# Moving 36 tile transposes from TensorE to the DMA crossbar, and the Q head masks from VectorE to GpSimd, in a transformer block bound by its exps

## The chip, the cores and the metric

One core of one Trainium2 chip. The metric is the device time of one execution in microseconds (us), as a median of several. Executions of one kernel mostly agree within 0.3%; each is marked fast or slow, and only fast ones are compared. Engines: PE is TensorE (matrix products and transposes), DVE is VectorE, ACT is ScalarE, POOL is GpSimd, SP is SyncE, which here only issues DMAs.

## The reference

A transformer block on one sequence of S = 2048 tokens, D = 512, with H = 32 heads of 16, and a gated FFN with F = 1792; all in bf16.

```python
def _A_ref(x, wqkv, wo):                       # attention
    qkv = (x @ wqkv).reshape(B, S, 3, H, Dh).transpose(2, 0, 3, 1, 4)
    q, k, v = qkv[0], qkv[1], qkv[2]
    scores = einsum("bhqd,bhkd->bhqk", q, k) * (Dh ** -0.5)
    p = softmax(scores)
    o = einsum("bhqk,bhkd->bhqd", p, v)
    return o.transpose(0, 2, 1, 3).reshape(B, S, D) @ wo
def _B_ref(x, w_gate, w_up, w_down):           # FFN
    return (gelu(x @ w_gate) * (x @ w_up)) @ w_down

h = x + _A_ref(layernorm(x), wqkv, wo)         # LN1
return h + _B_ref(layernorm(h), w_gate, w_up, w_down)   # LN2
```

With 32 heads of width 16, the scores are 2048 tiles of 128 keys x 512 queries, and every element needs an exp. That is the kernel's bulk.

## The kernel before

The kernel is a list scheduler in Python. Each piece of work is a generator that yields operations with a modelled duration, and asks for PSUM banks with `Acquire` (PSUM is the memory that PE's products are written to, here in eight banks of 128 x 512 floats); the scheduler decides, when the program is built, the order of the instructions on each engine. On the chip this order is fixed, and engines wait for one another by semaphores.

The exps are shared. ACT takes two tiles per step, from PSUM banks 0 to 3 (`pbank`), into `PT`:

```python
yield Op("act", TEXP(n), ACTF(PT[:, p0:p0 + n, :], pbank[:, b0:b0 + n, :], ACT.Exp, scale=LN2 / 1024, bias=math.log(PSCALE)), ...)
```

DVE takes the rest whenever the scheduler finds room, in groups of four tiles:

```python
# dconv, per tile: PSUM -> uint16
yield Op("dve", 0.603, lambda e: e.tensor_scalar(out=dXE[...][:, 0, j, :], in0=pbank[:, b, :], ...))
# dchain, per group of n tiles: mantissa, exponent, product
yield Op("dve", t1, lambda e: e.tensor_scalar(out=W.bitcast(U16), in0=X, ...), reads=kX, writes=kW, port=True)   # W is dW
yield Op("dve", t1, lambda e: e.tensor_scalar(out=E, in0=X, ...), reads=kX, writes=kE, port=True)
yield Op("dve", t2, lambda e: e.tensor_tensor(out=X.bitcast(F16), in0=W, in1=X.bitcast(F16), op=ALU.mult), reads=kW + kX, writes=kX, port=True)
```

So less other work on DVE lets the scheduler hand more tiles to DVE, and ACT gets fewer steps. Where PE would idle, the scheduler puts dummy matmuls (`zero_bf`).

Three kinds of tile are transposed by PE into a PSUM bank and copied out by DVE: the 16 tiles of LN1, the 16 of the attention output (`Otok`) and the 16 of LN2 (`hn_sb`, the same memory as `OnT`). One of them, the others look alike:

```python
b = yield Acquire(reads=rd, gate=lambda: C["oproj"] >= first_t[c])
pt = pbank[:, b, :].bitcast(BF16)
yield Op("pe", 4 * TTR, cols=512, fns=[lambda e, hc=hc: e.transpose(out=pt[:, 128 * hc:128 * hc + 128], in_=Otok[:, cp, qt, 128 * hc:128 * hc + 128], identity=ident[:])
                     for hc in range(4)], reads=rd, writes=[("pb", b)])
yield copy_op(c, qt, OnT[:, qt, :, :], pt[:, 0:512].rearrange("p (c s) -> p c s", c=4), reads=[("pb", b)], writes=[("OH", qt)])
```

Q leaves PSUM twice, since one matmul of 32 rows serves two heads of 16 and each head needs a copy in which the other's rows are zero:

```python
for par in range(2):
    ...                                        # (the first ones on ACT)
    yield Op("dve", 0.66, lambda e, par=par: e.tensor_scalar(out=QT[:, c, 2 * j + par, :], in0=pbank[:, b, :], scalar1=qmask[:, par:par + 1], scalar2=None, op0=ALU.mult), ...)
proj_done(b)
```

Of the kernel before, what the change touches and what calls it, by code (L numbers as in the profile page):

```python
# [1093 lines left out]
TAIL = dict(pe=0.17, act=0.13, dve=0.083)  # L1094
LATS = {("pe", "act"): 0.04, ("pe", "dve"): 0.04, ("act", "pe"): 0.058, ("dve", "pe"): 0.06, ("dve", "dve"): 0.034, ("act", "act"): 0.04, ("pool", "pool"): 0.05}
PVM = 2
SLOTS = ((0, 2), (2, 2))
PVB = 4
DENSE = (5, 6, 7)
# [62 lines left out]
def fast_path(nc, P, base0, ARENA, pbank, flag, A_x, A_wqkv, A_wo, B_x, B_w_gate, B_w_up, B_w_down, out):  # L1162
# [25 lines left out]
    xn_sb = at("xn_sb", [128, 8, D], BF16)  # L1188
    GUT = at("GUT", [128, NFC, 512], BF16, offE)
    offF = cur[0]  # L1190
    xnT = at("xnT", [128, 4, S], BF16)
    wqkv_sb = at("wqkv_sb", [128, 4, 3 * D], BF16)
    wg_sb = at("wg_sb", [128, 4, F], BF16, offF)
    wu_sb = at("wu_sb", [128, 4, F], BF16, offF + 14336)
# [14 lines left out]
    h_off = [h_at(c) for c in range(NC)]  # L1209
    h_over = [k for _, k in h_off]  # L1210
    h_c = [at("h_c%d" % c, [128, CHUNKS[c] // 128, D], BF16, h_off[c][0]) for c in range(NC)]
    hnT_c = [at("hnT_c%d" % c, [128, 4, CHUNKS[c]], BF16, h_off[c][0] + 4096) for c in range(NC)]
    Otok = at("Otok", [128, 2, 4, D], BF16)
    wo_sb = at("wo_sb", [128, 4, D], BF16)
    OnT = at("OnT", [128, 4, 4, 128], BF16)
# [40 lines left out]
    T0 = 12.0  # L1256
# [12 lines left out]
    def MM(o, l, r, start, stop, tile=None):  # L1269
        if tile is None:  # L1270
            return lambda e: e.matmul(o, l, r, start=start, stop=stop)  # L1271
        return lambda e: e.matmul(o, l, r, start=start, stop=stop, tile_position=tile)  # L1272
# [83 lines left out]
    def ln1_norm(c, t):  # L1356
# [13 lines left out]
                     reads=[xkey(c, t), ("rstd", t), ("nmr", t)], writes=[("xn", t % 8)], gate=ok)  # L1370
        sch.add(ln1_T(c, t), 2 + 7 * c)

    def ln1_T(c, t):
        b = yield Acquire(reads=[("xn", t % 8), "ident"])
        pt = pbank[:, b, :].bitcast(BF16)
        yield Op("pe", 4 * TTR, cols=512, fns=[lambda e, dc=dc: e.transpose(out=pt[:, 128 * dc:128 * dc + 128], in_=xn_sb[:, t % 8, 128 * dc:128 * dc + 128], identity=ident[:])
                             for dc in range(4)], reads=[("xn", t % 8), "ident"], writes=[("pb", b)])
        C[("xnT", t)] = 1
        o_ap, i_ap = xnT[:, :, 128 * t:128 * t + 128], pt[:, 0:512].rearrange("p (c s) -> p c s", c=4)
        yield Op("dve", 0.333, lambda e: e.tensor_copy(out=o_ap, in_=i_ap), reads=[("pb", b)], writes=[("xnT", t)])  # L1380
        sch.release(b)
        C["ln1"] += 1


    def proj_kq(items):
        for (which, j, c, dl) in items:
            base = 0 if which == "q" else D
            rd = [("w%s0" % which) if j == 0 else "wA" if which == "q" else "wB"] + [("xnT", t) for t in range(4 * c, 4 * c + 4)]
            me.prio = dl
            b = yield Acquire(reads=rd)  # L1390
            for hf in range(2):
                yield Op("pe", 2 * TMM, cols=1024, fns=[MM(pbank[:, b, :], wqkv_sb[:, dc, base + 128 * j:base + 128 * j + 128], xnT[:, dc, 512 * c:512 * c + 512], dc == 0, dc == 3)
                                                        for dc in (2 * hf, 2 * hf + 1)], reads=rd, writes=[("pb", b)])
            sch.add((q_evac if which == "q" else k_evac)(j, c, b, dl), dl)

# [12 lines left out]

    def q_evac(j, c, b, dl):

        for par in range(2):
            if par == 0 and dl < T0:
                yield Op("act", 0.47, lambda e: e.activation(out=QT[:, c, 2 * j, :], in_=pbank[:, b, :], func=ACT.Copy, scale=qmask[:, 0:1]),
                         reads=[("pb", b), ("qm", 0)], writes=[("qT", 2 * j, c)])
            else:
                yield Op("dve", 0.66, lambda e, par=par: e.tensor_scalar(out=QT[:, c, 2 * j + par, :], in0=pbank[:, b, :], scalar1=qmask[:, par:par + 1], scalar2=None, op0=ALU.mult),
                         reads=[("pb", b), ("qm", par)] + [("qT", 2 * j, c)] * par, writes=[("qT", 2 * j + par, c)])
        proj_done(b)

    def proj_v():  # L1420
        for t in range(NT):
            rd = ["wB", ("xnT", t)]
            mev.prio = T0 + 2 + 1.8 * t
            b = yield Acquire(reads=rd)
            for hf in range(2):
                yield Op("pe", 2 * TMM, cols=1024, fns=[MM(pbank[:, b, :], xnT[:, dc, 128 * t:128 * t + 128], wqkv_sb[:, dc, 2 * D:3 * D], dc == 0, dc == 3)
                                      for dc in (2 * hf, 2 * hf + 1)], reads=rd, writes=[("pb", b)])
            op = Op("dve", 0.605, lambda e, b=b, t=t: e.tensor_copy(out=VA[:, t, :, 0:16], in_=pbank[:, b, :].rearrange("p (h i) -> p h i", i=16)),
                    reads=[("pb", b)], writes=[("V", t)])
            sch.add(v_evac(op, b), mev.prio)  # L1430
# [287 lines left out]
    def post(c, qt):  # L1718
        cp, t = c % 2, first_t[c] + qt
        xi = t % 2  # L1720
        hh, hT = h_c[c], hnT_c[c]
        rd = [("Otok", cp, s) for s in range(NSLOT)] + ["ident"]
        b = yield Acquire(reads=rd, gate=lambda: C["oproj"] >= first_t[c])
        pt = pbank[:, b, :].bitcast(BF16)
        yield Op("pe", 4 * TTR, cols=512, fns=[lambda e, hc=hc: e.transpose(out=pt[:, 128 * hc:128 * hc + 128], in_=Otok[:, cp, qt, 128 * hc:128 * hc + 128], identity=ident[:])  # L1725
                             for hc in range(4)], reads=rd, writes=[("pb", b)])
        yield copy_op(c, qt, OnT[:, qt, :, :], pt[:, 0:512].rearrange("p (c s) -> p c s", c=4), reads=[("pb", b)], writes=[("OH", qt)])
        sch.release(b)
        b2 = yield Acquire(reads=[("OH", qt), "wo"])
        for hf in range(2):  # L1730
            yield Op("pe", 2 * TMM, cols=1024, fns=[MM(pbank[:, b2, :], OnT[:, qt, hc, :], wo_sb[:, hc, :], hc == 0, hc == 3) for hc in (2 * hf, 2 * hf + 1)],
                     reads=[("OH", qt), "wo"], writes=[("pb", b2)])
        dQ = P.retire(h_over[c])
        yield Op("dve", 0.605, lambda e: e.tensor_tensor(out=hh[:, qt, :], in0=pbank[:, b2, :], in1=xres[:, xi, :], op=ALU.add),
                 reads=[("pb", b2), ("xres", xi)], writes=[("h", c, qt)], extra=lambda: dQ)
        sch.release(b2)
        C["oproj"] += 1
        yield Op("dve", 0.605, lambda e: e.bn_stats(out=stats2[:, t, :], in_=hh[:, qt, :]), reads=[("h", c, qt)], writes=[("stats2", t)])
        yield Op("dve", 0.1, lambda e: e.bn_aggr(out=mv2[:, t, :], in_=stats2[:, t, :]), reads=[("stats2", t)], writes=[("mv2", t)])  # L1739
        tt_ = slice(t, t + 1)  # L1740
        yield Op("pool", 0.25, lambda e: e.tensor_scalar(out=rstd2[:, tt_], in0=mv2[:, t, 1:2], scalar1=EPS, scalar2=None, op0=ALU.add), reads=[("mv2", t)], writes=[("rstd2", t)])  # L1741
        yield Op("pool", 0.57, lambda e: e.tensor_tensor(out=rstd2[:, tt_], in0=rstd2[:, tt_], in1=nhalf[:, 0:1], op=ALU.pow), reads=[("rstd2", t), "nhalf"], writes=[("rstd2", t)])
        yield Op("dve", 0.327, lambda e: e.tensor_scalar(out=hn_sb[:, qt, :], in0=hh[:, qt, :], scalar1=mv2[:, t, 0:1], scalar2=rstd2[:, tt_], op0=ALU.subtract, op1=ALU.mult),
                 reads=[("h", c, qt), ("rstd2", t), ("mv2", t)], writes=[("OH", qt)], port=True)
        b3 = yield Acquire(reads=[("OH", qt), "ident"])
        pt3 = pbank[:, b3, :].bitcast(BF16)
        yield Op("pe", 4 * TTR, cols=512, fns=[lambda e, dc=dc: e.transpose(out=pt3[:, 128 * dc:128 * dc + 128], in_=hn_sb[:, qt, 128 * dc:128 * dc + 128], identity=ident[:])  # L1747
                             for dc in range(4)], reads=[("OH", qt), "ident"], writes=[("pb", b3)])
        yield copy_op(c, qt, hT[:, :, 128 * qt:128 * qt + 128], pt3[:, 0:512].rearrange("p (c s) -> p c s", c=4),
                 reads=[("pb", b3)], writes=[("hnT", c, qt)], extra=lambda: dQ)  # L1750
        sch.release(b3)
        C[("hnT", c)] = C.get(("hnT", c), 0) + 1
# [10 lines left out]
    def product(c, k, b, w, rd):  # L1763
        nq = CHUNKS[c]
        for j in range(pack(c)):
            fc = k * pack(c) + j
            for hf in range(2):
                yield Op("pe", 2 * tmm(nq), cols=2 * nq, fns=[MM(pbank[:, b, j * nq:j * nq + nq], w[:, dc, 128 * fc:128 * fc + 128], hnT_c[c][:, dc, :], dc == 0, dc == 3)
                                                              for dc in (2 * hf, 2 * hf + 1)], reads=rd, writes=[("pb", b)])

    def gates(c):
# [7 lines left out]
    def tmm(n):  # L1779
        return max(0.09, TMM * n / 512)  # L1780
# [173 lines left out]
```

## Time and profile before

| | before |
|---|---|
| median (first three runs) | 845.17 us |
| span of the profiled run | 843.2 us |
| ACT exp steps | 796, 742.3 us |
| what ACT waited ahead of them | 17.7 us |
| DVE busy | 769.0 us (91%) |
| PE busy | 819.5 us (97%), of it 203 dummies |

The page of the kernel before, its head; each engine's busy time, share of the span and instruction count:

```profile
span 843.2 us, 16693 instructions
PE 819.5 (97%) x6773; PEld 254.4 (30%) x6773; DVE 769.0 (91%) x1246; ACT 786.3 (93%) x833; POOL 42.9 (5%) x100
```

Its groups of instructions: line, engine, operation, output<-input, forms, count, then busy us and mean ns of one, then the idle time just before them and what ended most of it:

```profile
L1278 ACT ACTIVATE PT<-pbank 128x1024 bf16<-128x1024 f32 x796 | 742.3, 1072 | 17.7 <-PE pbank L1272 14.6
...
L1416 DVE TENSOR_SCALAR QT<-pbank,qmask 128x512 bf16<-128x512 f32 x31 | 22.9, 745 | 0.4
...
L1380 DVE COPY xnT<-pbank 128x512 bf16<-128x512 bf16 x16 | 6.5, 419 | 6.0 <-PE pbank L1376 5.9
L1716 DVE COPY hnT_c<-pbank 128x512 bf16<-128x512 bf16 x15 | 6.2, 417 | 0.4 <-PE pbank L1747 0.4
L1747 PE MATMUL pbank<-ident,OnT 128*128 128x128 bf16 x64 | 6.2, 221 | 0.9 <-DVE LCHK L1854 0.7
...
L1376 PE MATMUL pbank<-ident,xn_sb 128*128 128x128 bf16 x64 | 5.9, 220 | 1.2 <-POOL xn_sb L1369 1.2
L1716 DVE COPY OnT<-pbank 128x512 bf16<-128x512 bf16 x15 | 5.7, 415 | 0.7 <-PE pbank L1725 0.7
L1725 PE MATMUL pbank<-ident,Otok 128*128 128x128 bf16 x64 | 5.6, 220 | 0.0
```

The first line is the limit: 742.3 + 17.7 = 760.0 us of the span are exps or ACT waiting to start one. The other 83.2 us are the start before the first exp and the FFN's tail after the last, plus ACT's few other instructions. So **span = exps + waits ahead of exps + about 83 us**, and a change is read by its two movable terms. The other lines are what the change touches: 17.7 us of PE for 192 transposes (0.09 us each, as they overlap) and about 0.42 us of DVE for each copy.

Where do ACT's waits lie? The stretch from 20 to 80 us is called the ramp below. The windows view of before: window and its length, then busy us (and instructions) of PE, PEld, DVE, ACT, POOL, the granted PE clock, the DMA share and GB/s:

```profile
20.00:80.00 60.00, 58.58 (x393) 15.69 (x391) 43.63 (x77) 53.22 (x57) 15.42 (x39) 1.00 0.00 1
80.00:200.00 120.00, 117.73 (x904) 30.25 (x902) 118.11 (x182) 119.07 (x130) 0.00 (x0) 1.00 0.14 49
```

From 80 us on ACT is all but full. Between 20 and 80 us, while the late LN1 tiles and the projections still run, it idles 60 - 53.22 = 6.8 us. The timeline of ACT there (start, length, instructions; in brackets the idle time before and its releaser):

```profile
30.41 2.86 ACT L1278 ACTIVATE PT<-pbank 128x1024 bf16<-128x1024 f32 x3 [0.28 <-PE pbank L1272]
33.84 5.79 ACT L1278 ACTIVATE PT<-pbank 128x1024 bf16<-128x1024 f32 x6 [0.58 <-PE pbank L1272]
40.09 1.94 ACT L1278 ACTIVATE PT<-pbank 128x1024 bf16<-128x1024 f32 x2 [0.47 <-PE pbank L1272]
43.65 11.11 ACT L1278 ACTIVATE PT<-pbank 128x1024 bf16<-128x1024 f32 x12 [1.61 <-PE pbank L1272]
...
62.37 1.94 ACT L1278 ACTIVATE PT<-pbank 128x1024 bf16<-128x1024 f32 x2 [2.86 <-PE pbank L1272]
```

Seven waits for scores from PE, the longest 2.86 us at 62 us.

### The profile page before, as it was taken

Reading aid. Unit: us, or ns where it says so; the run is one execution under the profiler, and the core shown is the slowest. Engines: PE = TensorE matmul, PEld = TensorE weight load, DVE = VectorE, ACT = ScalarE, POOL = GpSimd, SP = SyncE. Lnnn points to the kernel's source line nnn. Section 1 sums busy time; section 2 is a strip of 40 time slices with the busy share of each in tenths; the row PEclk is TensorE's granted clock in tenths of the full one; section 3 lists DMA queues with packets and bytes.
Section 4 is the critical chain, followed back from the end, with each engine's and each line's share of the span. In section 5 each row is a group of like instructions: output and inputs, shape, how many; then the busy total and the mean of one; then the engine's idle time right before and its main releaser. Section 6 shows DMA issues by size and latency. Waiting matters only on the chain.

```text
span 843.2 us, 16693 instructions
## 1 busy us (share of the span) xinstructions
PE 819.5 (97%) x6773; PEld 254.4 (30%) x6773; DVE 769.0 (91%) x1246; ACT 786.3 (93%) x833; POOL 42.9 (5%) x100
## 2 busy tenths in 40 slices
PE   8999999999999999999999989999999989999997
PEld 3222222222222222222222222222233333333455
DVE  7569999999999999999989989999999999899862
ACT  3979999999999999999999999999999999999941
POOL 5600000000010000000010000000010000000000
PEclk9999999999999999999999999999999999999999
DMA  6000004300000000000000000000000000000000
GB/s 200 1 1 1 1 2 160 116 1 1 8 7 1 2 1 2 7 26 7 2 14 1 1 1 2 7 26 7 2 21 7 2 1 2 2 26 14 2 13 18
DMA packets 12327, 15.06 MB, mean 18 GB/s; under 512 B 1744, under 2 KB 11216, under 8 KB 12240
## 3 DMA queue, kind: packets, MB, share of 16 engines
q1 hardware_dynamic: 12240, 13.90, 5.0%
q8 instruction: 55, 0.90, 0.4%
q14 instruction: 32, 0.26, 0.1%
HBM read 11.80 MB, written 2.10 MB: 16 GB/s over the span
## 4 chain that ended last, share of the span: by engine, by line
PE 75%; ACT 12%; DVE 6%; issue 5%; POOL 1%; ACTq 0%; POOLq 0%; DVEq 0%
PE pbank L1272 46%; PE pbank L1271 21%; ACT PT L1278 11%; PE pbank L1870 3%; DVE dXE L1590 2%; DVE dXE L1607 1%; PE pbank L1275 1%; ACT GUT L1809 1%; PE pbank L1867 1%; PE pbank L1880 1%; DVE dXE L1605 1%; POOL xn_sb L1369 1%; DVE dW L1604 1%; PE pbank L1725 0%; PE pbank L1747 0%
## 5 line engine op out<-in xcount | busy, mean ns | idle before, releaser
L1278 ACT ACTIVATE PT<-pbank 128x1024 bf16<-128x1024 f32 x796 | 742.3, 1072 | 17.7 <-PE pbank L1272 14.6
L1272 PE MATMUL pbank<-QT,KT 32*128 32x512 bf16 x2048 | 345.0, 384 | 7.2 <-ACT PT L1278 4.9
L1590 DVE TENSOR_SCALAR dXE<-pbank 128x512 uint16<-128x512 f32 x456 | 296.9, 682 | 15.9 <-PE pbank L1272 12.8
L1272 PEld LDWEIGHTS pbank<-QT,KT 32*128 32x128 bf16 x2048 | 84.2, 91 | 311.5 <-ACT PT L1278 220.8
L1272 PE MATMUL pbank<-PT,VA 128*17 128x512 bf16 (+1 forms) x1992 | 149.4, 339 | 0.1
L1607 DVE TENSOR_TENSOR dXE<-dW,dXE 128x2048 f16<-128x2048 f16 (+1 forms) x115 | 139.1, 1210 | 2.0
L1604 DVE TENSOR_SCALAR dW<-dXE 128x2048 uint16<-128x2048 uint16 (+1 forms) x115 | 78.1, 679 | 0.8
L1605 DVE TENSOR_SCALAR dXE<-dXE 128x2048 uint16<-128x2048 uint16 (+1 forms) x115 | 78.1, 679 | 0.0
L1272 PE MATMUL pbank<-dXE,VA 128*17 128x512 f16 (+1 forms) x1136 | 70.3, 339 | 0.0
L1271 PE MATMUL pbank<-hnT_c,wu_sb 128*128 128x512 bf16 (+1 forms) x280 | 59.7, 346 | 7.4 <-DVE GUT L1823 6.8
L1271 PE MATMUL pbank<-hnT_c,wg_sb 128*128 128x512 bf16 (+1 forms) x280 | 65.5, 340 | 0.0
L1271 PE MATMUL pbank<-wd_sb,GUT 128*128 128x512 bf16 x224 | 59.2, 382 | 0.0
L1272 PEld LDWEIGHTS pbank<-PT,VA 128*17 128x17 bf16 x1992 | 39.2, 88 | 65.3 <-issue 57.8
L1870 PE MATMUL pbank<-ones_bf,zero_bf 128*128 128x512 bf16 x168 | 55.7, 386 | 0.0
L1823 DVE TENSOR_TENSOR GUT<-pbank,GUT 128x512 bf16<-128x512 f32 x56 | 37.3, 685 | 16.0 <-PE pbank L1271 12.8
L1741 POOL TENSOR_SCALAR rstd<-mv 128x1 f32<-128x1 f32 x16 | 6.6, 413 | 761.0 <-DVE mv L1739 761.0
L1271 PE MATMUL pbank<-xnT,wqkv_sb 128*128 128x512 bf16 x128 | 37.8, 383 | 0.0
L1271 PEld LDWEIGHTS pbank<-hnT_c,wu_sb 128*128 128x128 bf16 x280 | 23.5, 99 | 32.5 <-issue 11.8
L1797 DVE CAST GUT<-pbank 128x512 bf16<-128x512 f32 x49 | 33.1, 680 | 0.0
L1271 PEld LDWEIGHTS pbank<-hnT_c,wg_sb 128*128 128x128 bf16 x280 | 19.5, 97 | 27.8 <-issue 20.6
L1272 PEld LDWEIGHTS pbank<-dXE,VA 128*17 128x17 bf16 x1136 | 18.7, 88 | 29.8 <-issue 24.0
L1271 PEld LDWEIGHTS pbank<-wd_sb,GUT 128*128 128x128 bf16 x224 | 17.0, 97 | 27.0 <-issue 14.3
(82 smaller groups left out, 390.8 us busy)
## 6 DMA issues: line engine op xcount, KB each, us to landing
xres<-in_A_x_dram SPq DMA_DIRECT2D x16, 128.0 KB, 2.2
out_dram<-out_sb SPq DMA_DIRECT2D x16, 128.0 KB, 1.7
wg_sb<-in_B_w_gate_dram SPq DMA_DIRECT2D x1, 1792.0 KB, 7.1
wu_sb<-in_B_w_up_dram SPq DMA_DIRECT2D x1, 1792.0 KB, 11.2
wd_sb<-in_B_w_down_dram SPq DMA_DIRECT2D x1, 1792.0 KB, 17.4
x_sb<-in_A_x_dram SPq DMA_DIRECT2D x3, 512.0 KB, 8.3
wqkv_sb<-in_A_wqkv_dram SPq DMA_DIRECT2D x1, 896.0 KB, 7.5
x_sb<-in_A_x_dram SPq DMA_DIRECT2D x2, 256.0 KB, 2.9
```

The source lines that it names most:

```text
L1271: return lambda e: e.matmul(o, l, r, start=start, stop=stop)
L1272: return lambda e: e.matmul(o, l, r, start=start, stop=stop, tile_position=tile)
L1275: return lambda e: e.transpose(out=o, in_=i, identity=idn)
L1278: return lambda e: e.activation(out=o, in_=i, func=func, **kw)
L1369: lambda e: e.tensor_scalar(out=xn_sb[:, t % 8, :], in0=x_sb[:, t, :], scalar1=rstd[:, tt_], scalar2=htmp[:, tt_], op0=ALU.mult, op1=ALU.add),
L1590: yield Op("dve", 0.603, lambda e: e.tensor_scalar(out=dXE[G["k"] % NX][:, 0, j, :], in0=pbank[:, b, :], scalar1=XMIN + 1024.0 * CENTER, s ...
L1604: yield Op("dve", t1, lambda e: e.tensor_scalar(out=W.bitcast(U16), in0=X, scalar1=0x3ff, scalar2=0xb800, op0=ALU.bitwise_and, op1=ALU.bit ...
L1605: yield Op("dve", t1, lambda e: e.tensor_scalar(out=E, in0=X, scalar1=0x7c00, scalar2=0x8, op0=ALU.bitwise_and, op1=ALU.bitwise_or), reads ...
L1607: yield Op("dve", t2, lambda e: e.tensor_tensor(out=X.bitcast(F16), in0=W, in1=X.bitcast(F16), op=ALU.mult), reads=kW + kX, writes=kX, por ...
L1797: yield Op("dve", 0.6, lambda e: e.tensor_copy(out=o_ap, in_=i_ap), reads=[("pb", b)], writes=keys, extra=dE)
L1823: yield Op("dve", 0.6, lambda e: e.tensor_tensor(out=o_ap, in0=u_ap, in1=o_ap, op=ALU.mult), reads=[("pb", b)] + keys, writes=keys)
L1870: fill_op = Op("pe", TMM, lambda e: e.matmul(pbank[:, PVB, :], zero_bf[:], ones_bf[:], start=False, stop=False, skip_group_check=True), re ...
```

## The change

Its intent: take work from PE and DVE and give it to engines that are idle. SP issues a DMA that transposes a whole 128 x 512 tile on the DMA crossbar, SBUF to SBUF, in place of four PE transposes, a PSUM bank and a DVE copy. It does so for the attention output and LN2 of all query chunks but the last, and for the LN1 tiles 8 to 15. Q leaves PSUM in one plain DVE pass, which frees the bank earlier, and GpSimd makes the two masked copies. Layouts of `xnT` and `hnT_c` change so that a transposed tile is contiguous. The core of the diff:

```diff
+TURN_X = 2
+    def turn(o, i, key, reads, writes, **kw):
+        return Op("sp", 0.125, lambda e: e.dma_start_transpose(out=o, in_=i), reads=reads, writes=writes, dma=key, **kw)
 ...
     def ln1_T(c, t):
+        if c >= TURN_X:
+            yield turn(xnT[:, t, :, :], xn_sb[:, t % 8, :], ("xT", t % 8), [("xn", t % 8)], [("xnT", t)])
+            C[("xnT", t)] = 1
+            C["ln1"] += 1
+            return
         b = yield Acquire(reads=[("xn", t % 8), "ident"])
 ...
     def q_evac(j, c, b, dl):
+        if dl >= T0:
+            raw = QT[:, c, 2 * j + 1, :]
+            yield Op("dve", 0.605, lambda e: e.tensor_copy(out=raw, in_=pbank[:, b, :]), reads=[("pb", b)], writes=[("qraw", j, c)])
+            proj_done(b)
+            for par in range(2):
+                yield Op("pool", 0.85, lambda e, par=par: e.tensor_scalar(out=QT[:, c, 2 * j + par, :], in0=raw, scalar1=qmask[:, par:par + 1], scalar2=1.0, op0=ALU.mult, op1=ALU.mult), ...)
+            return
 ...
     def post(c, qt):
+        if c < NC - 1:
+            yield turn(OnT[:, qt, :, :], Otok[:, cp, qt, :], ("OT", qt), rd[:-1], [("OH", qt)], gate=lambda: C["oproj"] >= first_t[c])
+        else:
             (as before: PE transposes and a copy)
 ...
+        if c < NC - 1:
+            yield turn(hT[:, qt, :, :], hn_sb[:, qt, :], ("hT", qt), [("OH", qt)], [("hnT", c, qt)], extra=lambda: dQ)
+            C[("hnT", c)] = C.get(("hnT", c), 0) + 1
+            return
         b3 = yield Acquire(reads=[("OH", qt), "ident"])
```

Because the scheduler decides the rest, the built programs differ in more than these lines. Counted in the two built orders: PE has 144 transposes fewer and 17 dummies more (203 to 220), DVE has 36 copies fewer, 30 masked Q evictions fewer and 15 plain ones more, GpSimd 30 mask passes, SP 36 transposes. ACT's exp steps go from 796 to 793 and DVE's exponential tiles from 456 to 462.

More of the change, by code (lines that the diff above doesn't have):

```diff
@@ L1096 @@
 PVM = 2
+DMAX = 3
+TURN_X = 2
 SLOTS = ((0, 2), (2, 2))
@@ L1190, in fast_path @@
     offF = cur[0]
-    xnT = at("xnT", [128, 4, S], BF16)
+    xnT = at("xnT", [128, NT, 4, 128], BF16)
     wqkv_sb = at("wqkv_sb", [128, 4, 3 * D], BF16)
@@ L1211, in fast_path @@
     h_c = [at("h_c%d" % c, [128, CHUNKS[c] // 128, D], BF16, h_off[c][0]) for c in range(NC)]
-    hnT_c = [at("hnT_c%d" % c, [128, 4, CHUNKS[c]], BF16, h_off[c][0] + 4096) for c in range(NC)]
+    hnT_c = [at("hnT_c%d" % c, [128, CHUNKS[c] // 128, 4, 128], BF16, h_off[c][0] + 4096) for c in range(NC)]
     Otok = at("Otok", [128, 2, 4, D], BF16)
@@ L1378, in ln1_T @@
         C[("xnT", t)] = 1
-        o_ap, i_ap = xnT[:, :, 128 * t:128 * t + 128], pt[:, 0:512].rearrange("p (c s) -> p c s", c=4)
+        o_ap, i_ap = xnT[:, t, :, :], pt[:, 0:512].rearrange("p (c s) -> p c s", c=4)
         yield Op("dve", 0.333, lambda e: e.tensor_copy(out=o_ap, in_=i_ap), reads=[("pb", b)], writes=[("xnT", t)])
@@ L1391, in proj_kq @@
             for hf in range(2):
-                yield Op("pe", 2 * TMM, cols=1024, fns=[MM(pbank[:, b, :], wqkv_sb[:, dc, base + 128 * j:base + 128 * j + 128], xnT[:, dc, 512 * c:512 * c + 512], dc == 0, dc == 3)
+                yield Op("pe", 2 * TMM, cols=1024, fns=[MM(pbank[:, b, :], wqkv_sb[:, dc, base + 128 * j:base + 128 * j + 128], xnT[:, 4 * c:4 * c + 4, dc, :], dc == 0, dc == 3)
                                                         for dc in (2 * hf, 2 * hf + 1)], reads=rd, writes=[("pb", b)])
@@ L1409, in q_evac @@
     def q_evac(j, c, b, dl):
+        if dl >= T0:
[3 more added lines that the diff above has]
+            for par in range(2):
+                yield Op("pool", 0.85, lambda e, par=par: e.tensor_scalar(out=QT[:, c, 2 * j + par, :], in0=raw, scalar1=qmask[:, par:par + 1], scalar2=1.0, op0=ALU.mult, op1=ALU.mult),
+                         reads=[("qraw", j, c), ("qm", par)] + [("qT", 2 * j, c)] * par, writes=[("qT", 2 * j + par, c)] + [("qraw", j, c)] * par)
+            return
         for par in range(2):
@@ L1425, in proj_v @@
             for hf in range(2):
-                yield Op("pe", 2 * TMM, cols=1024, fns=[MM(pbank[:, b, :], xnT[:, dc, 128 * t:128 * t + 128], wqkv_sb[:, dc, 2 * D:3 * D], dc == 0, dc == 3)
+                yield Op("pe", 2 * TMM, cols=1024, fns=[MM(pbank[:, b, :], xnT[:, t, dc, :], wqkv_sb[:, dc, 2 * D:3 * D], dc == 0, dc == 3)
                                       for dc in (2 * hf, 2 * hf + 1)], reads=rd, writes=[("pb", b)])
@@ L1722, in post @@
         rd = [("Otok", cp, s) for s in range(NSLOT)] + ["ident"]
-        b = yield Acquire(reads=rd, gate=lambda: C["oproj"] >= first_t[c])
-        pt = pbank[:, b, :].bitcast(BF16)
-        yield Op("pe", 4 * TTR, cols=512, fns=[lambda e, hc=hc: e.transpose(out=pt[:, 128 * hc:128 * hc + 128], in_=Otok[:, cp, qt, 128 * hc:128 * hc + 128], identity=ident[:])
-                             for hc in range(4)], reads=rd, writes=[("pb", b)])
-        yield copy_op(c, qt, OnT[:, qt, :, :], pt[:, 0:512].rearrange("p (c s) -> p c s", c=4), reads=[("pb", b)], writes=[("OH", qt)])
-        sch.release(b)
+        if c < NC - 1:
+            yield turn(OnT[:, qt, :, :], Otok[:, cp, qt, :], ("OT", qt), rd[:-1], [("OH", qt)], gate=lambda: C["oproj"] >= first_t[c])
+        else:
+            b = yield Acquire(reads=rd, gate=lambda: C["oproj"] >= first_t[c])
+            pt = pbank[:, b, :].bitcast(BF16)
+            yield Op("pe", 4 * TTR, cols=512, fns=[lambda e, hc=hc: e.transpose(out=pt[:, 128 * hc:128 * hc + 128], in_=Otok[:, cp, qt, 128 * hc:128 * hc + 128], identity=ident[:])
+                                 for hc in range(4)], reads=rd, writes=[("pb", b)])
+            yield copy_op(c, qt, OnT[:, qt, :, :], pt[:, 0:512].rearrange("p (c s) -> p c s", c=4), reads=[("pb", b)], writes=[("OH", qt)])
+            sch.release(b)
         b2 = yield Acquire(reads=[("OH", qt), "wo"])
@@ L1748, in post @@
                              for dc in range(4)], reads=[("OH", qt), "ident"], writes=[("pb", b3)])
-        yield copy_op(c, qt, hT[:, :, 128 * qt:128 * qt + 128], pt3[:, 0:512].rearrange("p (c s) -> p c s", c=4),
+        yield copy_op(c, qt, hT[:, qt, :, :], pt3[:, 0:512].rearrange("p (c s) -> p c s", c=4),
                  reads=[("pb", b3)], writes=[("hnT", c, qt)], extra=lambda: dQ)
@@ L1767, in product @@
             for hf in range(2):
-                yield Op("pe", 2 * tmm(nq), cols=2 * nq, fns=[MM(pbank[:, b, j * nq:j * nq + nq], w[:, dc, 128 * fc:128 * fc + 128], hnT_c[c][:, dc, :], dc == 0, dc == 3)
+                yield Op("pe", 2 * tmm(nq), cols=2 * nq, fns=[MM(pbank[:, b, j * nq:j * nq + nq], w[:, dc, 128 * fc:128 * fc + 128], hnT_c[c][:, :, dc, :], dc == 0, dc == 3)
                                                               for dc in (2 * hf, 2 * hf + 1)], reads=rd, writes=[("pb", b)])
```

## The prediction

> **What bounds it now.** ScalarE, by the exps. The windows view shows ACT busy 19.6 to 20.0 of every 20 us from 80 us on; between 80 and 810 us it idles about 9 us in all. The groups view: 796 exps, 742.3 us, 0.93 us a step. Outside, ACT idles 13 us in 0-20, 7 us in 20-80 (projections, late LN1 tiles) and 28 us in the tail, which belongs to PE and DVE. PE is 97% busy, but with 203 dummy matmuls (67 us). DVE is 91% busy.
>
> **What the change moves** (instruction order of both builds, durations from the groups view).
> - PE loses 144 transposes (about 0.1 us each, 14 us) and gets 17 more dummies (6 us).
> - DVE loses 36 copies of 0.42 us (15 us); 30 masked evictions of 0.74 us become 15 plain ones of 0.68 us (12 us less); it takes 6 more tiles of the DVE exponential at 1.3 us (8 us more). Net 19 us less.
> - ACT: 796 to 793 exps, 2.8 us less. The freed DVE time mostly stays idle.
> - GpSimd gets 30 mask passes, about 0.77 us each, as its 128x512 LN1 pass takes now, behind all LN1 tiles. They share a port with DVE's fast modes: the Trainium skill, "SBUF — State Buffer", section "SBUF: two separate sides", calls it an exclusive lock held for a whole instruction; no run here shows it yet. I expect a few passes stretched to 2 us, without harm.
> - SP gets 36 crossbar transposes of 128 KB. The trace has none; plain 128 KB loads land in 2.2 us. The skill, "VectorE: DVE Perf Modes", "The three transpose paths", has 1.3 us for one 128x128 by crossbar. My estimate for four blocks: 3 us to landing, 1 to 1.3 us apart back to back.
>
> **How much is on the critical path.**
> - Otok and LN2: the first output projection of chunk 0 stands 5 exp steps after the last head transposes, about 4 us after Otok; the later ones have more. The first gate matmul has roughly 5 us after the last LN2 tile. At 3 us these fit; at 5 to 6 us PE, and with it ACT, would stall 1 to 3 us at up to 8 places.
> - Late LN1: the K projection of tiles 8-11 is needed after 16 exp steps. Tile 11 leaves GpSimd at 29.2 us (timeline), its copy ends at 30.1, K leaves PSUM at 33.3. With 3 us of transpose this slips 0.5 to 1 us; tiles 12-15 (38.9 us) come out even. Against it PE, which ACT waits for in 30-80 us, is rid of 32 transposes: gain 1 to 2 us.
> - Tail: the last chunk keeps its PE transposes; unchanged.
>
> Sum: 845.2 - 2.8 (exps) - about 1 (ramp, net) = 841.5 us, range 835 to 850. Faster by over 2%: 0.03; within 2%: 0.92; slower by over 2%: 0.05.
>
> **What would show it.** Exp group near 740 us; PE and DVE busy lower by about 8 and 19 us; DMA issues near 3 us for xnT, OnT, hnT; no PE wait on DMA over 1 us at the projections; the ACT wait near 33 us 1 us longer, the one near 43 us not; GpSimd busy 23 us longer.
>
> **What would make it wrong.** Transposes landing in 6 us or more, or serialising at over 2 us each: every engine's order is fixed, so PE stalls ahead of the scores and ACT starves (850 to 865 us). Mask passes blocked by DVE, or blocking it, so that a score waits for GpSimd. Or, the other way, shorter DVE and PE queues remove the small ACT waits after 80 us: up to 9 us more.

## More of the kernel before

A dozen constants steer the scheduler:

```python
LOOK = 0.12      # how much later an operation may be ready and still go first by priority
SLACK = 0.3
GLAST, AHEAD, ATAIL = 8, 12, 8     # (one line each in the kernel)
DGAP = 3.0       # least spacing of the groups of DVE exponentials
```

## The result, and the profile after

| | before | after |
|---|---|---|
| median of the runs taken together | 844.72 us (844.25 to 845.54, 4 runs) | 841.5 us (839.75 to 842.34, 4 runs) |
| ratio | | 0.9958 (0.9944 to 0.9972) |
| span of the profiled run | 843.2 us | 837.7 us |
| exp steps, busy | 796, 742.3 us | 793, 740.0 us |
| ACT's waits ahead of exps | 17.7 us | 14.5 us |
| DVE busy | 769.0 us | 755.5 us |

Ratios here and below are the mean time of one kernel's fast runs over that of the other's fast runs of the same rounds, so they are not quite the ratio of the medians; the range is a 95% interval. The changed kernel is 0.4% faster. Its profiled run was its fastest one (839.75 us), so the two spans differ by 5.5 us and the medians by only 3.2.

The page after, its head, and the groups that answer to those shown of before:

```profile
span 837.7 us, 16474 instructions
PE 802.0 (96%) x6582; PEld 245.4 (29%) x6654; DVE 755.5 (90%) x1210; ACT 784.1 (94%) x830; POOL 69.1 (8%) x130
```

```profile
L1280 ACT ACTIVATE PT<-pbank 128x1024 bf16<-128x1024 f32 x793 | 740.0, 1077 | 14.5 <-PE pbank L1274 11.3
...
L1426 POOL TENSOR_SCALAR QT<-QT,qmask 128x512 bf16<-128x512 bf16 x30 | 25.0, 835 | 77.6 <-DVE QT L1423 76.2
L1423 DVE CAST QT<-pbank 128x512 bf16<-128x512 f32 x15 | 10.2, 686 | 1.8 <-PE pbank L1273 1.6
...
L1390 DVE COPY xnT<-pbank 128x512 bf16<-128x512 bf16 x8 | 3.1, 417 | 1.0 <-PE pbank L1386 1.0
L1386 PE MATMUL pbank<-ident,xn_sb 128*128 128x128 bf16 x32 | 2.8, 219 | 0.0
L1772 PE MATMUL pbank<-ident,OnT 128*128 128x128 bf16 x8 | 0.8, 222 | 0.9 <-DVE LCHK L1879 0.7
L1746 PE MATMUL pbank<-ident,Otok 128*128 128x128 bf16 x8 | 0.6, 219 | 0.0
```

Both terms of the sum moved: exps 742.3 to 740.0 (-2.3), waits 17.7 to 14.5 (-3.2), together the 5.5 us of the span. PE's and DVE's own drops are larger and are not the gain: they were not the limit. (PE's 17.5 us less is also too much: the page has 6654 weight loads and only 6582 matmuls, so 72 matmul records are missing.)

The DMA issues view after (count, median us to landing; a transpose moves one 128 x 512 tile, 128 KB):

```profile
xres<-in_A_x_dram SPq DMA_DIRECT2D x16, 128.0 KB, 2.3
...
OnT<-Otok SPq DMA_TRANSPOSE x14, 2.5
hnT_c<-OnT SPq DMA_TRANSPOSE x14, 2.5
xnT<-xn_sb SPq DMA_TRANSPOSE x8, 2.4
```

The windows of after, and the timeline of ACT in the stretch that showed seven waits before:

```profile
20.00:80.00 60.00, 58.44 (x389) 14.72 (x391) 43.46 (x73) 56.41 (x62) 17.70 (x42) 1.00 0.09 19
80.00:200.00 120.00, 116.28 (x889) 29.64 (x898) 112.37 (x172) 119.14 (x129) 22.19 (x26) 1.00 0.14 49
```

```profile
33.60 7.44 ACT L1280 ACTIVATE PT<-pbank 128x1024 bf16<-128x1024 f32 x8 [1.38 <-PE pbank L1274]
43.21 21.50 ACT L1280 ACTIVATE PT<-pbank 128x1024 bf16<-128x1024 f32 x23 [2.17 <-PE pbank L1274]
```

Two waits are left of seven. The wait near 33 us, which ends with the K projection of LN1 tiles 8 to 11, has grown from 0.58 to 1.38 us, since its transposes now take 2.4 us. The one near 43 us has grown from 1.61 to 2.17. The four small ones and the 2.86 us at 62 us are gone. ACT is busy 56.41 us of the 60, against 53.22.

Whether the transposes cost anything at the chunks is read on SP and PE. SP after, at the first chunk's attention output, and PE at the first matmul that reads it:

```profile
218.86 5.13 SPq L1376 DMA_TRANSPOSE OnT<-Otok  x4
```

```profile
222.53 0.38 PE L1273 MATMUL pbank<-wo_sb,OnT 128*128 128x512 bf16 x1 [0.16 <-issue]
```

Four transposes hold SP for 5.13 us, 1.28 us each. The first lands about 2.5 us after 218.86, at 221.4, and is read at 222.53: 1.1 us to spare. PE's only wait on a transpose in the whole trace is 0.8 us, for an LN1 tile.

### The profile page after: what moved, and what is told of

It reads as the page before. It is cut to its first block, busy times and chain, and to the rows that moved or that the text cites. A ratio compares the mean times of both kernels' runs of the same rounds, so it can differ in the third digit from the quotient of the medians.

```text
span 837.7 us, 16474 instructions
## 1 busy us (share of the span) xinstructions
PE 802.0 (96%) x6582; PEld 245.4 (29%) x6654; DVE 755.5 (90%) x1210; ACT 784.1 (94%) x830; POOL 69.1 (8%) x130
## 4 chain that ended last, share of the span: by engine, by line
PE 65%; ACT 15%; DVE 11%; issue 6%; POOL 1%; DMA 1%; SPq 0%; ACTq 0%; POOLq 0%
PE pbank L1274 40%; PE pbank L1273 22%; ACT PT L1280 14%; DVE dXE L1608 4%; DVE dXE L1625 3%; PE pbank L1895 2%; DVE dW L1622 1%; DVE dXE L1623 1%; PE pbank L1277 1%; DMA x_sb<-in_A_x_dram 1%; ACT GUT L1834 1%; PE pbank L1905 1%; ACT L1280 0%; DMA xnT<-xn_sb 0%; POOL xn_sb L1371 0%
## 5 line engine op out<-in xcount | busy, mean ns | idle before, releaser
L1280 ACT ACTIVATE PT<-pbank 128x1024 bf16<-128x1024 f32 x793 | 740.0, 1077 | 14.5 <-PE pbank L1274 11.3
L1608 DVE TENSOR_SCALAR dXE<-pbank 128x512 uint16<-128x512 f32 x462 | 301.5, 685 | 18.5 <-PE pbank L1274 15.3
L1625 DVE TENSOR_TENSOR dXE<-dW,dXE 128x2048 f16<-128x2048 f16 (+2 forms) x118 | 141.5, 1199 | 1.9
L1622 DVE TENSOR_SCALAR dW<-dXE 128x2048 uint16<-128x2048 uint16 (+2 forms) x118 | 80.2, 680 | 1.1
L1623 DVE TENSOR_SCALAR dXE<-dXE 128x2048 uint16<-128x2048 uint16 (+2 forms) x118 | 79.7, 675 | 0.0
L1274 PE MATMUL pbank<-dXE,VA 128*17 128x512 f16 (+1 forms) x1152 | 72.1, 339 | 0.8 <-DVE dXE L1625 0.6
L1762 POOL TENSOR_SCALAR rstd<-mv 128x1 f32<-128x1 f32 x16 | 8.8, 550 | 651.8 <-DVE mv L1760 651.8
L1273 PE MATMUL pbank<-wd_sb,GUT 128*128 128x512 bf16 x204 | 54.9, 381 | 2.8 <-issue 2.7
L1848 DVE TENSOR_TENSOR GUT<-pbank,GUT 128x512 bf16<-128x512 f32 x56 | 37.3, 686 | 14.5 <-PE pbank L1273 10.5
L1895 PE MATMUL pbank<-ones_bf,zero_bf 128*128 128x512 bf16 x139 | 46.5, 385 | 2.1 <-issue 2.1
L1426 POOL TENSOR_SCALAR QT<-QT,qmask 128x512 bf16<-128x512 bf16 x30 | 25.0, 835 | 77.6 <-DVE QT L1423 76.2
```

The lines of the kernel that those rows point to most:

```text
L1273: return lambda e: e.matmul(o, l, r, start=start, stop=stop)
L1274: return lambda e: e.matmul(o, l, r, start=start, stop=stop, tile_position=tile)
L1280: return lambda e: e.activation(out=o, in_=i, func=func, **kw)
L1426: yield Op("pool", 0.85, lambda e, par=par: e.tensor_scalar(out=QT[:, c, 2 * j + par, :], in0=raw, scalar1=qmask[:, par:par + 1], scalar2= ...
L1608: yield Op("dve", 0.603, lambda e: e.tensor_scalar(out=dXE[G["k"] % NX][:, 0, j, :], in0=pbank[:, b, :], scalar1=XMIN + 1024.0 * CENTER, s ...
L1762: yield Op("pool", 0.25, lambda e: e.tensor_scalar(out=rstd2[:, tt_], in0=mv2[:, t, 1:2], scalar1=EPS, scalar2=None, op0=ALU.add), reads=[ ...
```

## The experiments

A prediction that held by a net of small terms may still be right by luck, so the question is which part of the change pays, and whether 0.4% is its worth at all. The theories follow. (In the expectations "theory W" is the first, the work that the order holds; "theory L" is luck of the order; "rival R" says that the Q part brings the ramp's gain.)

- **Parts.** The exp steps fall because DVE is rid of copies and masks; the ramp gains because PE and PSUM are rid of the late LN1 transposes. Each part alone should bring its share.
- **Rival: order.** The constants of the kernel before may have been chosen for its own order of instructions. Any change makes the scheduler deal a new order, and a new order alone moves the time by as much as the measured gain. Then single parts come out at random, and the measured 0.4% is the change's worth minus the loss of a lucky order (or plus the luck of the new one).
- **Q jam.** A sub-theory: without the Q part, the masked Q evictions on DVE block the exps.
- **Hidden latency.** The transposes cost nothing because each has just enough room; if they took twice as long, the kernel would stall.

### The Q part alone

```diff
-TURN_X = 2
+TURN_X = 4
-DGAP = 3.0
+DGAP = 3.1
 # post(): both crossbar branches off
-        if c < NC - 1:
+        if False:
```

(With DGAP 3.0 the order that comes out reads a PSUM bank inside an open accumulation group; hence 3.1.)

> Only the Q part of the change (all transposes on TensorE again), and the group spacing constant DGAP at 3.1 instead of 3.0, because at 3.0 this combination gives an order that the race check refuses. 795 exp steps against 796 before. Theory W (the time follows the work that the order holds: 0.93 us per exp step, plus the ACT waits of the first 80 us): one step less, -0.9 us, and ACT's idle time between 20 and 80 us as before (about 6.5 us), so ratio about 0.999. Rival R (the first 80 us got better because Q leaves PSUM in one DVE pass): ACT idle in 20-80 us near 3.5 us and ratio about 0.996. Rival L (luck of the order): a ratio anywhere in 0.995 to 1.005 that does not follow the step count.

Measured: 844.13 us, ratio 0.9994 (0.9981 to 1.0007). 795 steps, 741.6 us, waits 18.5. Between 20 and 80 us ACT idles 60 - 55.02 = 5.0 us (before 6.8). So some of the ramp's gain comes with the Q part, and other waits (7.0 us after 200 us, against 4.4) take it back. This run is at DGAP 3.1 and the ratio is to the kernel before at 3.0; the fair comparison, with before at 3.1, comes with the next orders below.

### The late LN1 tiles on the crossbar alone

```diff
 # q_evac
-        if dl >= T0:
+        if False:
 # post(): both crossbar branches off
-        if c < NC - 1:
+        if False:
```

> Only the late LN1 transposes on the crossbar; Q and the rest as before. 798 exp steps against 796. Theory W: 2 steps more, +1.9 us, and about 3 us less ACT waiting in 20-80 us because TensorE is rid of 32 transposes there: ratio about 0.9985. Rival R (Q did it): no gain in 20-80 us, ratio about 1.002. Rival L: no relation to the count.

Measured: 854.98 us, ratio 1.0122 (1.0107 to 1.0136): 1.2% **slower**. In 20 to 80 us ACT is busy 56.11 us, so the ramp's gain is there in full. But there are 798 steps (747.2 us), and between 80 and 200 us ACT is busy only 115.41 of 120. The windows view of this kernel shows where:

```profile
150.00:155.00 5.00, 4.05 (x25) 1.06 (x19) 4.99 (x9) 4.78 (x7) 0.00 (x0) 0.86 1.03 410
155.00:160.00 5.00, 5.00 (x27) 1.37 (x26) 4.20 (x8) 1.50 (x2) 0.00 (x0) 0.50 1.06 367
160.00:165.00 5.00, 4.47 (x42) 1.12 (x40) 4.33 (x8) 5.00 (x7) 0.00 (x0) 0.96 0.59 188
```

ACT does 1.50 us of work in the 5 us from 155 us, with the PE clock at 0.50. Just before, the timeline of its DVE has the last masked Q evictions between the exponential's PSUM passes:

```profile
148.74 1.53 DVE L1434 TENSOR_SCALAR QT<-pbank,qmask 128x512 bf16<-128x512 f32 x2
150.19 3.17 DVE L1608 TENSOR_SCALAR dXE<-pbank 128x512 uint16<-128x512 f32 x5
153.27 0.74 DVE L1434 TENSOR_SCALAR QT<-pbank,qmask 128x512 bf16<-128x512 f32 x1
153.93 0.68 DVE L1608 TENSOR_SCALAR dXE<-pbank 128x512 uint16<-128x512 f32 x1
154.53 0.74 DVE L1434 TENSOR_SCALAR QT<-pbank,qmask 128x512 bf16<-128x512 f32 x1
```

This is where the Q jam theory comes from. As it reads the trace, PE waits for PSUM banks that DVE frees late, its clock is halved, and ACT starves for 3.5 us. What is recorded: PE's waits there are short (0.18 and 0.40 us for DVE, 0.28 for ACT), and the clock falls between 153.5 and 154.0 us. The FFN's weights are being loaded at the same time (DMA share 1.03 to 1.06), but they are also loaded between 140 and 155 us in before and in after, with the PE clock at 1.00, so the load by itself does not bring the jam.

### The attention output and LN2 on the crossbar alone

```diff
-TURN_X = 2
+TURN_X = 4
 # q_evac
-        if dl >= T0:
+        if False:
```

> Only the attention output and LN2 transposes on the crossbar. 794 exp steps. Theory W: 2 steps less, -1.9 us, the first 80 us as before: ratio about 0.998. If the crossbar transposes stall TensorE at the projections (they land after 2.5 us, one every 1.2 us), waits of TensorE on DMA over 0.5 us and a ratio above 1.0. Rival L: no relation to the count.

Measured: 846.26 us, ratio 1.0017 (1.0004 to 1.003). 794 steps, 741.3 us, two steps fewer for 28 DVE copies less (but the kernel with late LN1 alone lost 8 copies and has two steps more, so the count does not follow the copies alone); waits 20.0 us. The ramp is that of before (53.19 us busy, the same seven waits).

### Both crossbar parts, Q as before

```diff
 # q_evac
-        if dl >= T0:
+        if False:
```

> Both kinds of transposes on the crossbar, Q evicted from PSUM in two DVE passes as before. 791 exp steps against 796 before and 793 in the full change. Theory W: 5 steps less, -4.7 us, and -3 us in 20-80 us: ratio about 0.991, faster than the full change. Rival R: the 20-80 us gain is lost without the Q part, ratio about 0.9945. Rival L: no relation to the count, e.g. slower than the full change's 0.9958.

Measured: 847.26 us, ratio 1.0027 (1.0012 to 1.0043). Only 791 steps (738.6 us), fewer than the whole change, and the ramp is good (56.05 us busy), but waits are 21.5 us: the same jam at 150 to 165 us, with the same 3.5 us wait, and 7.4 us of small waits after 200 us.

So against before as it was, no part alone is clearly faster, the transposes together are slower, and yet the whole is 0.4% faster. The parts' shares do not add up: 0.9994 x 1.0122 x 1.0017 = 1.0133, against 0.9958. (The first factor is a kernel at DGAP 3.1 over one at 3.0, so the product mixes two settings; at equal settings it comes out otherwise, see below.) That fits the order theory, or the Q jam theory (the transposes pay only if the Q evictions get out of the way). The next runs decide between them: the same code with one constant of the scheduler nudged, which changes nothing but the order.

### Another order: DGAP 3.1, in three kernels

```diff
-DGAP = 3.0
+DGAP = 3.1
```

In the kernel before:

> The kernel before with one constant of its scheduler changed (DGAP 3.1 for 3.0): the same work, another order, 799 exp steps for 796. If the order matters little beyond the step count (theory W): +2.8 us, ratio 1.003. If the kernel before is a lucky order (theory L): the difference is larger or smaller than that by several us, with clock dips or waits at other places; a shift of over 4 us either way shows that reordering alone is worth as much as the whole change.

In the changed kernel:

> The changed kernel with the same constant at 3.1: 795 steps for 793. Theory W: about 1.9 us slower than the changed kernel, ratio to before 0.998, and about 3 to 5 us faster than before_d31. Theory L: no fixed gap to before_d31; if it is slower than before_d31, the change's gain is luck of the order.

In the kernel with both crossbar parts and the old Q:

> Transposes on the crossbar, Q in two DVE passes, DGAP 3.1 (793 steps, as many as the changed kernel). At 3.0 this kernel lost 3.5 us in one jam at 156 us, where three Q evictions of 0.74 us stood before exponential tiles on DVE while TensorE starved and its granted clock fell to 0.5. If that jam comes from keeping Q on DVE (theory Q), it is here too: a wait of ACT of 2 us or more between 80 and 200 us, ratio 1.0 or above. If it was luck of that order (theory L), ACT's idle time in 80-200 us is near 1 us and the ratio near 0.996.

Measured: before 850.34 us, ratio 1.0068 (1.0055 to 1.0082); after 839.8 us, 0.9947 (0.9933 to 0.996); crossbar parts alone 845.76 us, 1.001 (0.9996 to 1.0024). So the same nudge costs the kernel before 0.7% and the changed one nothing. With this setting the change is worth 10.5 us, of which 9.3 us lie in the span (847.3 to 838.0 us, medians of the runs' spans); the rest lies outside the profiled span and was not traced. The crossbar kernel keeps its jam (3.5 us at 159 us); but its order turned out to be the same as without the nudge over PE's first 3697 matmuls (counted in the built programs), far past the jam, so it is no independent draw. Nor is the kernel with the late LN1 tiles alone: its PE order is that of these two over the first 1515 matmuls, and DVE's lines at the jam are the same. The three jams are one order, seen three times.

The kernel with the Q part alone was also at DGAP 3.1, so this is its fair comparison:

```profile
L1278 ACT ACTIVATE PT<-pbank 128x1024 bf16<-128x1024 f32 x799 | 744.9, 1069 | 18.4 <-PE pbank L1272 15.1
L1280 ACT ACTIVATE PT<-pbank 128x1024 bf16<-128x1024 f32 x795 | 741.6, 1066 | 18.5 <-PE pbank L1274 15.6
```

(Groups view, before at 3.1, then the Q part alone; the ratios are to before as tuned, each on its own chip.) Against before at 3.1 the Q part alone is faster by 0.7% (0.9994 over 1.0068 is 0.9926) and the crossbar parts alone by 0.6% (0.9942). The product, 0.9869, is close to the whole change's 0.9880: at this one setting the parts do add up. The two traces have a gain of only 2.7 us for the Q part (846.5 to 843.8 us), against 6.2 us between the medians; before's profile was its fastest run, and that of the Q part one of its slower ones.

### Another order: SLACK 0.31, in three kernels

```diff
-SLACK = 0.3
+SLACK = 0.31
```

In the kernel before:

> The kernel before with another scheduler constant moved (SLACK 0.31 for 0.30): 800 exp steps for 796, an order that differs from the third microsecond of scores on. If the gain of the change is in the work and the kernel before is a lucky order (theory W+L): slower than before by 3 to 8 us, ratio 1.004 to 1.010. If it is luck alone (theory L): anywhere, also faster than before.

In the changed kernel:

> The changed kernel with SLACK 0.31: 792 steps for 793. Theory W+L: within 3 us of the changed kernel and 6 to 12 us faster than before_s31. Theory L: the gap to before_s31 is not repeated, it is under 4 us or reversed.

In the kernel with both crossbar parts and the old Q, where this nudge changes PE's order from its 763rd matmul on, before the jam:

> Transposes on the crossbar, Q in two DVE passes, SLACK 0.31: 794 steps. The run at DGAP 3.1 had the same order up to the jam at 156 us, so it did not test it; this one differs well before. Theory Q (the jam comes from Q on DVE): ACT waits 2 us or more in one piece between 80 and 200 us, and 5 us or more slower than after_s31. Theory L: no such wait, and within 3 us of after_s31.

Measured: before 849.24 us, 1.0047 (1.003 to 1.0063); after 840.71 us, 0.9954 (0.9938 to 0.9971); crossbar parts alone 842.39 us, 0.9973 (0.9956 to 0.9989). The third is the telling one. With the old Q evictions in place, ACT is busy 119.35 of 120 us between 80 and 200 us, so there is no jam:

```profile
80.00:200.00 120.00, 116.57 (x879) 29.26 (x887) 117.13 (x180) 119.35 (x129) 0.00 (x0) 1.00 0.14 49
```

The Q jam theory falls: the old Q evictions do not bring the jam by themselves, it came with one order. (The kernel before has them too, and none of its three orders jams.) The nine numbers together (ratios to the kernel before as it was; for the profiles, us of exps + ACT's waits for PE at exps in 20 to 80, 80 to 200 and 200 to 790 us):

| | before | crossbar parts only | whole change |
|---|---|---|---|
| as tuned | 1: 742.3 + 6.5, 0.7, 4.4 | 1.0027: 738.6 + 4.8, 4.1, 7.4 | 0.9958: 740.0 + 3.5, 0, 4.5 |
| DGAP 3.1 | 1.0068: 744.9 + 7.5, 0.7, 4.1 | 1.0010: 738.9 + 3.9, 4.4, 6.0 | 0.9947: 739.5 + 4.4, 0, 5.4 |
| SLACK 0.31 | 1.0047: 745.3 + 7.4, 0.4, 8.3 | 0.9973: 741.3 + 4.8, 0.4, 8.8 | 0.9954: 738.4 + 4.4, 0.8, 5.1 |
| mean | 1.0038: 744.2 + 7.1, 0.6, 5.6 | 1.0003: 739.6 + 4.5, 3.0, 7.4 | 0.9953: 739.3 + 4.1, 0.3, 5.0 |

The profiles in the SLACK row need care: those of before and of the crossbar parts fell on the longest run of their kernel (852.66 and 847.2 us, against medians of 849.24 and 842.39), so their waits after 200 us, 8.3 and 8.8, are more than is usual.

What follows. The whole change is faster than before at each of the three settings, by 0.4, 1.2 and 0.9%; 0.9953 over 1.0038 is a mean of 0.85%. Two of its terms are steady: exps 744.2 to 739.3 us and the ramp's waits 7.1 to 4.1 us, and the crossbar parts alone have nearly all of both (739.6 and 4.5). The other two columns are waits that come and go with the order. At equal settings the crossbar parts alone are 0.3% slower, 0.6% faster and 0.7% faster than before; only the slower one is set against before as tuned. Before as tuned has the fewest exps of its three orders and nearly the fewest waits: on these three orders, part of the change's worth was spent on losing that.

Counting without running agrees. I let the scheduler alone deal 240 orders of each kernel, with ten of its constants at random, and counted the exp steps (no time comes of this): a mean of 797.1 before and 790.5 after. The order of before, with 796, is a little better than its mean; that of after, with 793, a little worse than its own. Such draws include orders with LOOK below 0.12, which have the fault that is told under the last experiment. A recount (60 orders of each) gave 797.5 and 790.0; without the 21 faulty ones of each, 798.8 and 791.9, which says the same.

### Every transpose twice

The order is kept; behind each crossbar transpose SP issues it once more, to the same place, after the first has landed, and readers wait for the second.

```diff
+    def again(o, i, key, reads, writes, extra=()):
+        was = sch.done[P.last_writer[writes[0]]]     # the plan does not know of it
+        sch.done[P.dma("sp", lambda e: e.dma_start_transpose(out=o, in_=i), key, reads=reads, writes=writes, extra_deps=extra)] = was
```

> The changed kernel with every crossbar transpose issued twice into the same place, the second after the first has landed; the order on the other engines is that of the changed kernel. A transpose then lands about 5.0 us after its issue and the queue passes one every 3.7 us. Theory W: at 2.5 us they just fit, at 5 us they do not: about 3 us of TensorE waiting per chunk at the output projections, 4 to 5 us at the first gate matmul, about 2.5 us at each of the two late K projections: 20 to 35 us slower than the changed kernel, ratio 1.02 to 1.04 to before. Rival: transposes are off the critical path with room to spare, under 5 us slower, ratio below 1.002.

Measured: 898.56 and 899.55 us in the two fast runs; two more, at 912.21 and 912.55 us with a lower clock, count as slow (the median of all four is 905.88). The fast mean of 899.1 over the 844.77 median of before is about 1.064. The profile, of a fast run, has a span of 897.5 us, 59.8 above that of after. The exps stay at 793 steps (744.9 us), and the waits are 68.9 us. The two worst of them are at the K projections of the late LN1 tiles, on ACT's timeline:

```profile
42.36 7.44 ACT L1280 ACTIVATE PT<-pbank 128x1024 bf16<-128x1024 f32 x8 [9.93 <-PE pbank L1274]
56.86 7.44 ACT L1280 ACTIVATE PT<-pbank 128x1024 bf16<-128x1024 f32 x8 [7.06 <-PE pbank L1274]
```

And what the engines waited for, of its waits view (us in total, times, longest):

```profile
DVE h_c L1761 <- DMA xres<-in_A_x_dram: 13.4, 5, 4.2
PEld pbank L1273 <- DMA OnT<-Otok: 13.4, 9, 2.2
PE pbank L1273 <- DMA OnT<-Otok: 11.1, 8, 1.9
PE pbank L1273 <- DMA xnT<-xn_sb: 10.8, 2, 6.6
PE pbank L1273 <- DMA hnT_c<-OnT: 9.2, 3, 5.2
```

So the transposes have little room: once each they are all but hidden, and twice each they cost 59.8 us. The run doubles the time to landing and the time on SP's queue together, so it does not tell which of the two counts. The cost is about twice what I had expected. Two things had been left out. The plain residual loads (`xres`) stand behind the transposes in SP's queue, and DVE waits 13.4 us for them. And the granted PE clock is lower (0.961 on the mean of this run, 0.998 after); how much of the 59.8 us that is was not separated.

### Five constants picked for the changed kernel

If before has a lucky or tuned order and after has not, a better order for after should exist. This one was picked by counting steps.

```diff
-LOOK, GLAST, AHEAD, ATAIL, DGAP = 0.12, 8, 12, 8, 3.0
+LOOK, GLAST, AHEAD, ATAIL, DGAP = 0.11, 7, 13, 9, 3.1     # (one line each in the kernel)
```

> The changed kernel with five scheduler constants moved (LOOK 0.11, GLAST 7, AHEAD 13, ATAIL 9, DGAP 3.1), the setting of 240 random ones whose plan ends first: 786 steps for 793. Theory W: 7 steps, -6.5 us against the changed kernel, 835 us, ratio 0.988 if its waits stay at 14 us. If the order's waits decide (theory L): no better than the changed kernel, ratio 0.994 to 1.0.

Measured: 837.02 us, 0.9903 (0.9886 to 0.9919), with 786 steps (734.5 us), and a **wrong result**: relative error 0.0294. So this is not a version that beats anything. The time is told only for what it shows of the span's rule (734.5 + 18.6 + 82.3 = 835.4).

The cause was found without the chip. A simulation of this program's values gives the same relative error, 0.0294, and 0.0166 for the changed kernel; so the program itself is wrong, the same way each time. Taking back one constant at a time, only LOOK matters: with 0.12 the values are right, and the changed kernel with LOOK 0.11 alone is wrong as well. The built order shows why. All groups of DVE exponentials share the scratch tile `dW`. With LOOK 0.11, the first pass of a group (which writes `dW`) is put between the first pass and the product of the group before it, for 21 of the 120 groups, and the earlier group is multiplied with the later one's mantissas. Every semaphore is right, so a check for races has nothing to find; and the keys of the dependency tracker only order a read behind the last write, whoever made it. In the orders of before, after, and those with DGAP 3.1 or SLACK 0.31 of both, and of the crossbar kernel with SLACK 0.31, no group overlaps. With LOOK back at 0.12 the picked constants give 792 steps, so most of the seven steps saved came of the fault. That version was not run.

## Why the prediction was right, point by point

- **The limit** was named rightly: ACT's exps and its waits ahead of them make up the span in every profile.
- **Exps**: predicted -2.8 us, measured 742.3 to 740.0, -2.3.
- **Ramp**: predicted about -1 net, measured -3.0 (waits in 20 to 80 us, 6.5 to 3.5). The mis-sized term is "gain 1 to 2 us" for PE's relief. The wait near 33 us grew by 0.8 us, as predicted; but the relief took away the 2.86 us wait at 62 us and four small ones too, 4.3 us in all. The prediction also said that the wait near 43 us would not grow; it grew by 0.56 us.
- **Transposes**: my estimate was 3 us to landing and 1 to 1.3 us apart; the trace has 2.4 to 2.5, and 1.28. They fit where the prediction said they would, with 1.1 us to spare at the first output projection.
- **Mask passes**: predicted 0.77 us each with a few stretched to 2 us; the trace has a median of 0.692 and a longest of 1.656, and GpSimd is 26.2 us busier (predicted 23). No exp was seen to wait for one.
- **DVE**: predicted 19 us less busy, measured 13.5. The extra exponential tiles cost 10.7 us and not 8 (the four groups of `dXE` and `dW` together); the rest of the difference, 2.8 us, was not traced. It lies off the limit.
- **PE**: predicted 8 us less, the page says 17.5, of which an unknown part is missing records.
- **The number**: 841.5 was predicted and is the median. That this is exact is luck: the profile's gain is 5.5 us, the medians' 3.2, and the sum had 3.8.
- **"What would make it wrong"**: 5 to 6 us of landing was said to give 850 to 865 us. Doubling the transposes gave 899.1 in the fast runs, so the warning was right in kind and too small: it counted PE's stalls at the chunks and neither the loads queued behind on SP nor the clock.
- **What the prediction did not see**: that a part of the change's worth goes into replacing an order that was better than its neighbours (by the three orders run, and the counts). Measured against before at the same three settings, the change is worth 0.4, 1.2 and 0.9%. It put the gain down to counts from the one built order, which is why it met the measured number and not the change's worth.

Still open: how much the Q part adds. Alone, at DGAP 3.1, it is worth 0.7%, in one order. On top of the crossbar parts the whole change is at 0.9953 and these alone at 1.0003 on the mean, but two of those three orders share the jam; in the third, the Q part adds 0.2% (0.9954 against 0.9973). The rest of the difference (waits after 200 us of 7.4 against 5.0) falls where the last Q tile, masked at 140 us, is long past, and one profile of the three was of an unusually long run. It may be the order's luck.

## What to carry to other kernels

When a scheduler deals the order, one build of each version compares orders as much as ideas: nudge a constant that should not matter, in both versions, and compare at equal settings before crediting or blaming a part. Moving transposes to the DMA crossbar frees a PSUM bank, PE and DVE at once, but only where some 2.5 us of latency and 1.3 us of queue time per tile have room, and what stands behind them in the same queue waits too. And a freer choice of order needs a guard of its own for shared scratch: a check for races passes an order that is properly synchronised and wrong.

## What the Trainium skill lacked or had wrong

- "VectorE: DVE Perf Modes", section "The three transpose paths", gives 1309 ns for a 128 x 128 block by crossbar. It has no figure for a larger tile: here four blocks in one DMA land in 2.5 us (2.4 to 4.3), not in four times that. For TensorE it gives 390 ns per 128 x 128; here such a transpose is recorded at about 220 ns, and of many in a row each cost about 0.09 us of PE.
- "Advanced Engine Details and Errata", section "DMA Advanced Topics", says that transposing DMAs on TRN2 are as fast as regular ones. For landing this nearly holds (2.5 us against 2.3 for a plain 128 KB load). It lacks the queue's side: a transpose holds SP for 1.19 to 1.30 us, and a plain `xres` load for a median of 0.44 (0.33 at the least; 9.1 for one that stood behind the weight loads). Back to back, 128 KB per 1.28 us is about 102 GB/s, by my division, against the page's expected 350 to 400.
- "SBUF — State Buffer", section "SBUF: two separate sides", states the exclusive lock between DVE and GpSimd. The cost it gives is of a DMA issued from GpSimd (620 ns alone, 3100 beside a DVE copy); it has none for a computing instruction of GpSimd. Here a 0.69 us mask pass was stretched to 1.656 us at most, and 0.835 on the mean of 30; no run took DVE away to prove that the lock is the cause.
- "TensorE: Matmul & The Clock Gate", section "Part 1: The HAM clock gate", ties the half clock to an idle window of about 3.4 us, and describes shorter idle times that bring it too. Here a PE idle time of 2.66 us in the kernel before (ending at 499.90 us) was followed by a granted clock of 0.66 over 500 to 505 us, and one of 2.56 us in the kernel after (ending at 689.97) by 0.66 over 690 to 695. In the kernel with late LN1 alone, the clock was 1.00 up to 153.5 us, 0.59 over the next half us and then 0.50; in the 3.5 us before, PE was busy 2.73 us and no idle time shown was longer than 0.40 us.
